# A fused attention and two-MLP kernel: the second four units of the first group take their decays from stored sums of log a

## The chip, the cores and the metric

The kernel runs on one core of one Trainium2 chip. The metric is the device time of a run in microseconds (us). Three runs of the kernel before were timed; the median counts. A profiled execution, with a time of its own, gives the trace.

## The reference, cut to what matters

The input goes through attention with a decay, then through two MLPs.

```python
# x: (4, 8, 768, 32)   a: (4, 8, 768)   B, C: (4, 8, 768, 16)
log_a = np.log(np.clip(a, 1e-06, 1.0))
for c in range(nc):                                # chunks of 32
    cum = np.cumsum(la, axis=-1)
    L = np.exp(cum[:, :, :, None] - cum[:, :, None, :]) * causal
    M = einsum('bhin,bhjn->bhij', Cc, Bc) * L
    y[:, :, sl] = M @ xc + einsum('bhin,bhnd->bhid', Cc, state) * exp(cum)
    state = exp(sum(la)) * state + sum_j Bx        # Bx decayed from j to the chunk's end
x = y.transpose(0, 2, 1, 3).reshape(3072, 256)
h = np.maximum(np.maximum(x @ w1, x @ w2), x @ w3)  # 256 -> 768
x = h @ w_out                                       # 768 -> 256
h = x @ w_in                                        # 256 -> 2048, then P(h)/Q(h)
out = g @ w_out                                     # 2048 -> 256
```

The kernel works in chunks of 128 (`CH`), which gives the same values.

## The kernel before, in words

The sequence of 768 is cut into six groups of 128 (`NG`). A group holds eight units (`NU`): a unit u is one batch and one half of the heads, that is four heads with a 128 x 128 block each, laid side by side as 128 x 512. For each unit TensorE makes the decay exponents d (`d_mm`), ScalarE takes their exponential e, TensorE makes the products s of C and B for a pair of units (`s_mm`), VectorE multiplies s and e to m (`m_op`), and TensorE multiplies m by x into y (`y_intra`). After the third y of a group the state is made (`state`), and from the second group on the old state is added (`y_inter`), behind a product p of the stored sums (`prep`).

The exponents come in two ways. In the first group (units 0 to 7) VectorE multiplies a triangle by log a into a tile `tl` of float32, and TensorE multiplies another triangle by it: a float32 product of 128 x 512. In all later groups the sums of log a up to each place, which ScalarE and VectorE made once as three bfloat16 parts (`cs`), are stored in DRAM (`cum_d`) and loaded back by `load_cum` into one of two tiles `lr`: its fixed part `lrc` (192 KB of ones, minus ones and zeros) is loaded once for each tile, and four small loads bring a group's sums, one of 24 KB for `rd` and three of 16 KB for `ld`. Then one bfloat16 product of 128 x 512 gives the exponents. Three more small loads fill `re` for p. Both ways begin with a bfloat16 product of the mask `trib`.

Beside the attention, 20 pieces of weights of 512 KB each are loaded into three buffers `wraw` and turned from float64 words to a high and a low float32r part: two instructions on ScalarE, three on VectorE, two half-sized on GpSimd, one copy on ScalarE, two half-sized on GpSimd. Eight further pieces (`wo2`) follow. The MLPs need these parts; their products are float32r triples (`mm3`).

A planner (`Plan`) sets the order on every engine: each operation is recorded with a cost, and the list is put out in an order that follows from these costs, from due times (`at`) and from rings of buffers. So each engine runs one fixed list in order. `FIRST` names loads whose due time is set ahead of all others, in its own order. All loads and stores go through SyncE's queue (SPq), in one order, and take eight completion semaphores in turn: an entry of the queue is issued only when the eighth entry ahead of it has landed. A weight piece is also held until its buffer is free, which the third VectorE instruction of the piece three earlier ends. When the attention's last operation has been put out (`second`), its buffers are given to the MLPs, and they begin (L650 to L652).

In the timeline, d is at L488 (mask) and L490 (sums), tl at L494, e at L504, s at L477, m at L509, y at L520, the state at L555 and L566, p at L455, the weights' instructions at L246 to L262, the loads at L283 and L241.

Of the kernel before, what the change touches and what calls it, by code (L numbers as in the profile page):

```python
# [9 lines left out]
F32 = mybir.dt.float32  # L10
# [18 lines left out]

OL = 6
LEAD = 3
HV, HL = "HAHP", "HHKK"
WARM = 9
PIECE = 2.6
FIRST = ["a", "t", "b0", "z0", "n0", "x0", "w1"]
KD = DM // 128
NU = 2 * NB
F1 = DF1 // 128  # L40
# [10 lines left out]
class Plan:  # L51
# [16 lines left out]
    def op(self, engine, cost, fn, reads=(), writes=(), at=None, behind=()):  # L68
        i = len(self.ops)
        deps, after = set(), {w for t in behind for w in t.writers}  # L70
        for t in reads:
            assert (t.writers or t.given) and not t.closed
            deps.update(t.writers)
            t.readers.append(i)
        for t in writes:
            assert not t.closed
            if t.first is None:
                t.first = i
                if t.before and not t.before.given:
                    after.add(t.before.first)  # L80
                if t.prev:
                    t.prev.closed = True
                    deps.update(t.prev.writers + t.prev.readers)
            deps.update(t.writers + t.readers)
            t.writers.append(i)
        deps.discard(i)
        after.discard(i)
        self.ops.append((engine, cost, fn, [t for t in writes if t.first == i], deps, after, at,
                         self.phase))
# [67 lines left out]
def decay_attention_max_moe_rational_moe(  # L157
# [113 lines left out]
    op = plan.op  # L271
# [144 lines left out]
    op("act", 0.21, lambda: act.activation(out=wrev, in_=pw.t[:, 0:192], func=AF.Exp), [pw], [wrev_t])  # L416
    load(lambda: cum_d.rearrange("p q r i -> r (p q) i"), cs.rearrange("r p q i -> r (p q) i"), [cum_t], [cs_t], kb=295)

    for i in (1, 0):
        op("dve", 0.5, lambda i=i: dve.memset(lr[i][64:128].bitcast(F32), 0.0), [], [lr_t[i]])  # L420
        load(lambda i=i: lr[i][0:64], lrc, [lr_t[i]], kb=197, nm=f"l{i}")
    load(lambda: co_raw, coef, [co_t, own_t], kb=68)

    def load_cum(g):
        q, i, j = g // 3, g % 2, g % 3
        load(lambda: rd[i][0:24], cum_d[:, q].rearrange("p (g u f) i -> p g u (f i)", u=NU, g=3)[:, j],
             [rd_t[i]], [cum_t, lr_t[i]], kb=25)
        for p in range(3):
            load(lambda p=p: ld[i][24 + 4 * p:28 + 4 * p],
                 cum_d[p, q].rearrange("(g u f) j -> g f u j", u=NU, g=3)[j], [ld_t[i][p]], [cum_t, lr_t[i]], kb=16)  # L430
        for p in range(3):
            load(lambda p=p: re[i][8 * p:8 * p + 8].rearrange("h (b i) -> h b i", b=NB),
                 cum_d[p, q].rearrange("(g b h) i -> g h b i", b=NB, g=3)[j], [re_t[i][p]], [cum_t], kb=16)

# [16 lines left out]
    def prep(g):  # L451
        if g:
            p0 = new("pd", "d", 2)
            book(("p0", g), 0.22)
            op("pe", 0.22, lambda: pe.matmul(p0.t, sel, re[g % 2], start=True, stop=True),  # L455
               [sel_t, *re_t[g % 2]], [p0], when["p0", g])
            e0[g] = new("s2", "e0", 2)
            op("act", 0.59, lambda: act.activation(out=e0[g].t, in_=p0.t, func=AF.Exp), [p0], [e0[g]])
            op("pool", 1.4, lambda: pool.tensor_tensor(out=ctg[g].t, in0=ctg[g].t, in1=e0[g].t, op=ALU.mult),
               [e0[g]], [ctg[g]])  # L460
        if g < NG - 1:
            op("dve", 0.8, lambda: dve.tensor_tensor(
                out=bg[g].t, in0=bg[g].t,
                in1=wrev[:, 32 * g:32 * g + 32].rearrange("j (u f) -> j u f", f=4)[:, :, None, :].to_broadcast(
                    [128, NU, NS, 4]), op=ALU.mult),
               [wrev_t], [bg[g]])
# [15 lines left out]
    def d_mm(u):  # L482
        g, k = divmod(u, NU)
        t = new("pd", "d", 2)

        def mm(w, x):

            pe.matmul(t.t.rearrange("j (f i) -> j f i", f=4), trib[:, 0],  # L488
                      trib[:, 1:2].to_broadcast([128, 4, CH]), start=True, stop=False)
            pe.matmul(t.t, w(), x(), start=False, stop=True)  # L490
        if g == 0:

            tl = new("s2", "tl", 2)
            op("dve", 0.78, lambda: dve.tensor_tensor(  # L494
                out=tl.t.rearrange("t (f i) -> t f i", f=4), in0=tri_s[:, 0:1, :].to_broadcast([128, 4, CH]),
                in1=la[:, 4 * u:4 * u + 4, None].to_broadcast([128, 4, CH]), op=ALU.mult), [tri_t, la_t], [tl])
            book(("d", u), 1.08)
            op("pe", 1.08, lambda: mm(lambda: tri_s[:, 1, :], lambda: tl.t), [tri_t, trib_t, tl], [t], when["d", u])
        else:
            book(("d", u), 0.46)  # L500
            op("pe", 0.46, lambda: mm(lambda: ld[g % 2][:, k], lambda: rd[g % 2]),
               [trib_t, lr_t[g % 2], rd_t[g % 2], *ld_t[g % 2]], [t], when["d", u])
        e_t[u] = e = new("s4", "e", 4)
        op("act", 0.59, lambda: act.activation(out=e.t, in_=t.t, func=AF.Exp), [t], [e])  # L504
# [88 lines left out]
    for g in range(2):  # L593
        load_s(g)
        load_v(g)
    prep(0)
    load_cum(1)
    for s in range(NS_ALL + LEAD + 3):
        if s < NS_ALL:
# [368 lines left out]
```

## Time and profile before

| | |
|---|---|
| median of 3 runs | 578.93 us (577.61 to 580.32) |
| profiled execution: its time | 579.21 us |
| profiled execution: span from first to last instruction | 577.3 us |
| TensorE (PE) busy | 556.8 us, 96% |
| VectorE (DVE) busy | 511.9 us, 89% |
| GpSimd (POOL) busy | 440.6 us, 76% |
| ScalarE (ACT) busy | 435.3 us, 75% |
| attention (until the first MLP product) | 0 to 100.4 us |

The profiled execution's own time lies 1.9 us above its span and 0.3 us above the median of the runs. PE is TensorE's matmuls, PEld its weight loads, SPq the queue of SyncE. Matmuls overlap: a matmul of 128 x 512 shows 0.38 to 0.39 us of busy time, but the next one starts sooner than that, so the time that one takes is read from start to start.

### The profile page before, as it was taken

Reading aid. Unit: us, or ns where it says so; the run is one execution under the profiler, and the core shown is the slowest. Engines: PE = TensorE matmul, PEld = TensorE weight load, DVE = VectorE, ACT = ScalarE, POOL = GpSimd, SP = SyncE. Lnnn points to the kernel's source line nnn. Section 1 sums busy time; section 2 is a strip of 40 time slices with the busy share of each in tenths; the row PEclk is TensorE's granted clock in tenths of the full one; section 3 lists DMA queues with packets and bytes.
Section 4 is the critical chain, followed back from the end, with each engine's and each line's share of the span. In section 5 each row is a group of like instructions: output and inputs, shape, how many; then the busy total and the mean of one; then the engine's idle time right before and its main releaser. Section 6 shows DMA issues by size and latency. Waiting matters only on the chain.

```text
span 577.3 us, 8164 instructions
## 1 busy us (share of the span) xinstructions
PE 556.8 (96%) x2747; PEld 411.2 (71%) x2758; DVE 511.9 (89%) x777; ACT 435.3 (75%) x756; POOL 440.6 (76%) x410
## 2 busy tenths in 40 slices
PE   8989989989999999999999999999999999999997
PEld 3333433768787788888888888888888888886563
DVE  7888979777999999998889988898898889988996
ACT  4677768556888878878788787778777877778883
POOL 1756767887989967778677877687777997869883
PEclk9999999999999999999999999999999999999999
DMA  6877864533000000101000010000000010000000
GB/s 216 243 270 238 237 233 148 182 110 109 1 1 2 18 20 0 37 1 38 0 1 37 1 33 6 0 20 18 1 1 1 0 37 0 1 1 36 2 0 36
DMA packets 19047, 33.71 MB, mean 58 GB/s; under 512 B 3526, under 2 KB 4030, under 8 KB 19006
## 3 DMA queue, kind: packets, MB, share of 16 engines
q1 hardware_dynamic: 19003, 33.20, 17.9%
q8 instruction: 21, 0.34, 0.2%
q14 instruction: 23, 0.16, 0.1%
HBM read 27.27 MB, written 5.91 MB: 57 GB/s over the span
## 4 chain that ended last, share of the span: by engine, by line
PE 53%; DVE 17%; POOL 17%; issue 4%; ACT 4%; DMA 3%; SPq 2%; POOLq 0%; ACTq 0%; DVEq 0%
PE pg L650 7%; PE pg L652 7%; PE pg L651 6%; PE ph L650 5%; PE ph L652 5%; PE ph L651 5%; PE po L652 4%; PE po L650 4%; PE po L651 4%; POOL glo L853 2%; PE s L477 2%; DMA wraw<-in_w_dram 2%; POOL v L819 2%; POOL hlo L295 2%; DVE pr L845 2%
## 5 line engine op out<-in xcount | busy, mean ns | idle before, releaser
L853 POOL TENSOR_TENSOR glo<-w,ghi 128x512 fp32r<-128x512 f32 x80 | 105.5, 1319 | 16.2 <-ACT ghi L196 16.1
L650 PE MATMUL pg<-xhi,w_hi 128*128 128x512 f32 x202 | 79.1, 392 | 2.8 <-DVE xa L732 2.2
L652 PE MATMUL pg<-xhi,w_lo 128*128 128x512 f32 x202 | 78.8, 390 | 0.0
L651 PE MATMUL pg<-xlo,w_hi 128*128 128x512 f32 x202 | 78.7, 390 | 0.0
L840 ACT ACTIVATE pr<-v,qc 128x512 f32<-128x512 f32 x83 | 57.4, 693 | 22.2 <-DVE v L826 11.3
L295 POOL TENSOR_TENSOR hlo<-xa,hhi 128x512 fp32r<-128x512 f32 x36 | 49.5, 1376 | 26.0 <-ACT hhi L196 25.9
L258 POOL TENSOR_TENSOR wa<-wa,we 128x256 uint32<-128x256 uint32 x56 | 44.2, 800 | 32.9 <-DVE wa L253 32.9
L196 ACT ACTIVATE ghi<-w 128x512 fp32r<-128x512 f32 x80 | 50.4, 630 | 23.9 <-PE po L652 14.2
L650 PE MATMUL ph<-yhi,win_hi 128*128 128x512 f32 x160 | 62.7, 392 | 1.7 <-DVE w L838 1.5
L651 PE MATMUL po<-glo,wo_hi 128*128 128x512 f32 x160 | 62.4, 390 | 0.4 <-POOL glo L853 0.4
L652 PE MATMUL ph<-yhi,win_lo 128*128 128x512 f32 x160 | 62.3, 390 | 0.0
L650 PE MATMUL po<-ghi,wo_hi 128*128 128x512 f32 x160 | 62.3, 390 | 0.0
L652 PE MATMUL po<-ghi,wo_lo 128*128 128x512 f32 x160 | 62.3, 390 | 0.0
L651 PE MATMUL ph<-ylo,win_hi 128*128 128x512 f32 x160 | 62.3, 389 | 0.0
L845 DVE SCALAR_TENSOR_TENSOR pr<-w,co,pr 128x512 f32<-128x512 f32 x83 | 61.9, 746 | 0.0
L819 POOL TENSOR_TENSOR v<-t,v 128x512 f32<-128x512 f32 x44 | 58.1, 1320 | 2.8
L842 DVE SCALAR_TENSOR_TENSOR v<-v,pr 128x512 f32<-128x512 f32 x83 | 56.2, 677 | 2.2 <-ACT pr L841 2.2
L847 DVE SCALAR_TENSOR_TENSOR w<-v,pr 128x512 f32<-128x512 f32 x83 | 56.3, 678 | 0.4
L841 ACT ACTIVATE pr<-pr 128x512 f32<-128x512 f32 x86 | 50.5, 587 | 0.9
L732 DVE TENSOR_TENSOR xa<-xa,pg 128x512 f32<-128x512 f32 x67 | 45.5, 679 | 2.3 <-PE pg L652 2.1
L650 PEld LDWEIGHTS pg<-xhi,w_hi 128*128 128x128 f32 x202 | 37.9, 188 | 12.1 <-DVE xa L732 3.1
L837 POOL TENSOR_TENSOR w<-w,t 128x512 f32<-128x512 f32 x20 | 25.9, 1293 | 24.0 <-DVE v L826 22.1
(167 smaller groups left out, 1485.1 us busy)
## 6 DMA issues: line engine op xcount, KB each, us to landing
wraw<-in_wo_dram SPq DMA_DIRECT2D x11, 512.0 KB
wraw<-in_w_dram SPq DMA_DIRECT2D x9, 512.0 KB
wraw<-in_win_dram SPq DMA_DIRECT2D x8, 512.0 KB
xn<-in_xn_dram SPq DMA_DIRECT2D x6, 512.0 KB
out_dram<-ob SPq DMA_DIRECT2D x12, 256.0 KB
xt_d<-xo SPq DMA_DIRECT2D x10, 256.0 KB
xst<-xt_d SPq DMA_DIRECT2D x10, 256.0 KB
bt<-in_bz_dram SPq DMA_DIRECT2D x6, 256.0 KB
```

Source lines behind the costliest of these rows:

```text
L196: act.activation(out=o, in_=i, func=AF.Copy)
L295: lambda: e.tensor_tensor(out=lo.t, in0=src(), in1=hi.t.bitcast(F32), op=ALU.subtract),
L650: pe.matmul(dst, wh, hi, start=first, stop=False)
L651: pe.matmul(dst, wh, lo, start=False, stop=False)
L652: pe.matmul(dst, wl, hi, start=False, stop=last)
L819: pop(1.23, lambda: pool.tensor_tensor(out=f(v), in0=f(t1), in1=f(v), op=ALU.mult), [t1], [v])
L840: aop(0.62, lambda: act.activation(out=f(r), in_=f(v), func=AF.Ln, bias=qc), [v], [r])
L841: aop(0.48, lambda: act.activation(out=f(r), in_=f(r), func=AF.Exp, scale=-1.0), [], [r])
L842: dop(0.61, lambda: dve.scalar_tensor_tensor(out=f(v), in0=f(v), scalar=QC, in1=f(r), op0=ALU.add, op1=ALU.mult), [r], [v])
L845: dop(0.61, lambda: dve.scalar_tensor_tensor(out=f(r), in0=f(w), scalar=c(0), in1=f(r), op0=ALU.add, op1=ALU.mult), [w], [r])
L847: dop(0.61, lambda: dve.scalar_tensor_tensor(out=f(w), in0=f(v), scalar=2.0, in1=f(r), op0=ALU.subtract, op1=ALU.mult), [v, r], [w])
L853: pop(1.23, lambda: pool.tensor_tensor(out=f(lo), in0=f(w), in1=f(hi).bitcast(F32), op=ALU.subtract), [w, hi], [lo])
```

## The change

Units 0 to 3 keep the triangle's product. Units 4 to 7 of the first group take the stored sums, as all later groups do: `load_cum(0)` is called, with due times ahead of others ("r0" in `FIRST`), and without the `re` loads, which the first group has no use for. The fixed part for the first group's tile, "l0", is put ahead of the first group's bn. The two memsets of `lr` move from VectorE to GpSimd, and the order of the two tiles is turned.

```diff
+ND = 4
-FIRST = ["a", "t", "b0", "z0", "n0", "x0", "w1"]
+FIRST = ["a", "t", "b0", "z0", "l0", "n0", "x0", "w1", "r0"]
...
-    for i in (1, 0):
-        op("dve", 0.5, lambda i=i: dve.memset(lr[i][64:128].bitcast(F32), 0.0), [], [lr_t[i]])
+    for i in (0, 1):
+        op("pool", 0.9, lambda i=i: pool.memset(lr[i][64:128].bitcast(F32), 0.0), [], [lr_t[i]])
         load(lambda i=i: lr[i][0:64], lrc, [lr_t[i]], kb=197, nm=f"l{i}")
...
     def load_cum(g):
         load(lambda: rd[i][0:24], cum_d[:, q].rearrange("p (g u f) i -> p g u (f i)", u=NU, g=3)[:, j],
-             [rd_t[i]], [cum_t, lr_t[i]], kb=25)
+             [rd_t[i]], [cum_t, lr_t[i]], kb=25, nm=f"r{g}" if not g else None)
         for p in range(3):
             load(lambda p=p: ld[i][24 + 4 * p:28 + 4 * p],
-                 cum_d[p, q].rearrange("(g u f) j -> g f u j", u=NU, g=3)[j], [ld_t[i][p]], [cum_t, lr_t[i]], kb=16)
-        for p in range(3):
+                 cum_d[p, q].rearrange("(g u f) j -> g f u j", u=NU, g=3)[j], [ld_t[i][p]], [cum_t, lr_t[i]], kb=16,
+                 nm=f"r{g}" if not g else None)
+        for p in range(3 if g else 0):
...
-        if g == 0:
+        if u < ND:
             tl = new("s2", "tl", 2)
...
     prep(0)
+    load_cum(0)
     load_cum(1)
```

Because a planner sets the order, the change moves instructions on all engines. First SyncE's queue, from the load of the second group's bt on; `lr_125` is the first group's tile in the change, `lr_126` and `cz_135` are the second group's. Before:

```order
L283 DMA bt<-in_bz_dram 128x512
L283 DMA cz_135<-in_ct_dram 32x512
L283 DMA re_128<-cum_d 8x4x128 x3
L241 DMA wraw<-in_w_dram 128x2x512
L283 DMA cz_135<-in_ct_dram 32x512 x3
L283 DMA xn<-in_xn_dram 128x1024
L283 DMA lr_126<-cum_d 24x1x512
L283 DMA lr_126<-cum_d 4x8x128 x3
L283 DMA bn<-in_bn_dram 128x512
L283 DMA ct<-in_ct_dram 128x512
L241 DMA wraw<-in_w_dram 128x2x512
```

With the change:

```order
L285 DMA bt<-in_bz_dram 128x512
L285 DMA cz_135<-in_ct_dram 32x512
L285 DMA lr_125<-cum_d 24x1x512
L285 DMA lr_125<-cum_d 4x8x128 x3
L243 DMA wraw<-in_w_dram 128x2x512
L285 DMA re_128<-cum_d 8x4x128 x3
L285 DMA lr_126<-cum_d 24x1x512
L285 DMA lr_126<-cum_d 4x8x128 x2
L243 DMA wraw<-in_w_dram 128x2x512
L285 DMA lr_126<-cum_d 4x8x128
L285 DMA cz_135<-in_ct_dram 32x512 x3
L285 DMA xn<-in_xn_dram 128x1024
```

Four new loads stand ahead of the fourth weight piece. The fifth piece now stands ahead of the last three loads of `cz_135`, of xn, bn and ct; before it stood behind them all.

On TensorE, the middle of the first group, before: products of tl for units 3 to 5 between s and y.

```order
L477 MATMUL s<-cz_134,bt 128x512 x2
L488 LDWEIGHTS trib
L488 MATMUL d<-trib 128x512
L490 MATMUL d<-tl,tri_s 128x512
L488 LDWEIGHTS trib
L488 MATMUL d<-trib 128x512
L490 MATMUL d<-tl,tri_s 128x512
L520 MATMUL y<-m,xn 32x128 x8
L488 LDWEIGHTS trib
L488 MATMUL d<-trib 128x512
L490 MATMUL d<-tl,tri_s 128x512
L477 MATMUL s<-cz_134,bt 128x512 x2
```

With the change, from unit 3's product on:

```order
L493 MATMUL d<-tl,tri_s 128x512
L523 MATMUL y<-m,xn 32x128 x4
L480 MATMUL s<-cz_134,bt 128x512 x2
L523 MATMUL y<-m,xn 32x128 x4
L480 MATMUL s<-cz_134,bt 128x512 x2
L523 MATMUL y<-m,xn 32x128 x8
L480 MATMUL s<-cz_134,bt 128x512 x2
L491 LDWEIGHTS trib
L491 MATMUL d<-trib 128x512
L493 LDWEIGHTS lr_125
L493 MATMUL d<-lr_125 128x512
```

All of the first group's s and y of units 0 to 3 now come ahead of unit 4's d.

Last, TensorE where the second group's first s (it reads `cz_135`) is reached. Before, three d of the second group and y of units 4 to 6 stood ahead of it:

```order
L490 MATMUL d<-lr_126 128x512
L520 MATMUL y<-m,xn 32x128 x4
L488 LDWEIGHTS trib
L488 MATMUL d<-trib 128x512
L490 LDWEIGHTS lr_126
L490 MATMUL d<-lr_126 128x512
L520 MATMUL y<-m,xn 32x128 x4
L488 LDWEIGHTS trib
L488 MATMUL d<-trib 128x512
L490 LDWEIGHTS lr_126
L490 MATMUL d<-lr_126 128x512
L520 MATMUL y<-m,xn 32x128 x4
```

With the change it follows the first group's last d (unit 7), ahead of p and of every d of the second group:

```order
L523 MATMUL y<-m,xn 32x128 x4
L491 LDWEIGHTS trib
L491 MATMUL d<-trib 128x512
L493 LDWEIGHTS lr_125
L493 MATMUL d<-lr_125 128x512
L480 MATMUL s<-cz_135,bt 128x512 x2
L458 LDWEIGHTS sel
L458 MATMUL d<-re_128,sel 128x512
L523 MATMUL y<-m,xn 32x128 x4
```

## Rows read from the trace of the kernel before

**Rows 1.** Stretches: length, busy PE, PEld, DVE, ACT, POOL, clock, DMA share, GB/s
```profile
0.00:100.00 100.00, 88.65 (x745) 37.26 (x756) 86.57 (x151) 70.61 (x127) 61.96 (x78) 1.00 0.73 228
100.00:160.00 60.00, 55.83 (x240) 44.58 (x241) 47.28 (x64) 39.83 (x71) 51.58 (x57) 0.97 0.29 98
160.00:540.00 380.00, 379.07 (x1657) 310.35 (x1656) 346.44 (x511) 299.97 (x514) 301.68 (x251) 1.00 0.04 12
```

**Rows 2.** Timeline of TensorE: a float32 unit and the instruction behind it, then a bfloat16 unit
```profile
10.95 0.39 PE L488 MATMUL d<-trib 128*128 128x512 bf16 x1
11.18 1.02 PE L490 MATMUL d<-tl,tri_s 128*128 128x512 f32 x2
12.13 1.13 PE L477 MATMUL s<-cz,bt 64*128 64x512 f32 x4
...
24.78 0.39 PE L488 MATMUL d<-trib 128*128 128x512 bf16 x1
...
25.32 0.43 PE L520 MATMUL y<-m,xn 128*32 128x128 f32 x8
```

**Rows 3.** Timeline of VectorE: tl of units 4 to 7, and one memset of lr
```profile
4.78 0.70 DVE L420 MEMSET lr<- 64x768 f32 x1 [0.21 <-issue]
...
13.03 0.68 DVE L494 TENSOR_TENSOR tl<-tri_s,la 128x512 f32<-128x512 f32 x1
...
14.84 2.06 DVE L494 TENSOR_TENSOR tl<-tri_s,la 128x512 f32<-128x512 f32 x2
...
18.09 1.22 DVE L494 TENSOR_TENSOR tl<-tri_s,la 128x512 f32<-128x512 f32 x1
```

**Rows 4.** Timeline of TensorE at the start: the warming products ahead of the first real ones
```profile
2.29 4.02 PE L376 MATMUL y<-zero 128*128 128x512 bf16 x9 [2.29 <-DVE zero L372]
...
6.11 1.06 PE L399 MATMUL s<-tri_s,la 128*96 128x128 f32 x4
```

**Rows 5.** Timeline of SyncE's queue: start and time of issue (landing comes later)
```profile
10.23 1.04 SPq L241 DMA_DIRECT2D wraw<-in_w_dram  x2
...
14.81 0.40 SPq L241 DMA_DIRECT2D wraw<-in_w_dram  x1
16.89 2.12 SPq L283 DMA_DIRECT2D cz<-in_ct_dram  x3
...
22.69 0.38 SPq L241 DMA_DIRECT2D wraw<-in_w_dram  x1
...
69.25 0.35 SPq L283 DMA_DIRECT2D lr<-cum_d  x1
```

**Rows 6.** Waits of SyncE's queue: in total, times, longest
```profile
SPq L283 <- DMA wraw<-in_w_dram: 4.7, 4, 2.5
```

**Rows 7.** Timeline of PEld: p of the fifth group, after the load at 69.25
```profile
70.46 0.09 PEld L455 LDWEIGHTS <-sel 24*128 24x128 bf16 x1 [0.76 <-DMA lr<-cum_d]
```

**Rows 8.** Timeline: the second group's first s, and the standstill behind it
```profile
26.57 1.13 PE L477 MATMUL s<-cz,bt 64*128 64x512 f32 x4
...
28.98 0.66 ACT L249 ACTIVATE we<-wraw 128x512 uint32<-128x512 uint32 x1 [2.71 <-DMA wraw<-in_w_dram]
...
30.18 0.38 PE L488 MATMUL d<-trib 128*128 128x512 bf16 x1 [1.07 <-ACT e L504]
```

**Rows 9.** Two stretches with that standstill, columns as in rows 1
```profile
25.00:30.00 5.00, 3.97 (x35) 1.28 (x35) 2.38 (x3) 2.29 (x5) 3.65 (x4) 1.00 0.94 225
30.00:35.00 5.00, 3.64 (x27) 1.31 (x26) 4.29 (x9) 4.08 (x9) 1.59 (x2) 1.00 0.57 199
```

**Rows 10.** Timeline of TensorE: its longest wait in the first MLP
```profile
125.80 0.50 PE L650 MATMUL pg<-xhi,w_hi 128*128 128x512 f32 x1 [1.94 <-DVE xa L732]
```

**Rows 11.** The three stretches behind that wait, columns as in rows 1
```profile
126.00:128.00 2.00, 2.00 (x8) 1.58 (x8) 0.64 (x2) 1.45 (x3) 1.58 (x2) 0.79 0.21 71
128.00:130.00 2.00, 2.00 (x7) 1.52 (x6) 1.56 (x3) 0.63 (x1) 1.31 (x2) 0.50 0.50 192
130.00:132.00 2.00, 2.00 (x9) 1.64 (x8) 1.81 (x4) 1.81 (x4) 0.38 (x1) 0.86 0.00 0
```

## The prediction

> **What bounds the kernel now.** I read first the stretches of the span. After 160 us TensorE is busy for 379.07 of 380 us, and the change touches nothing there: what it is worth is decided earlier. The attention (0 to 100 us) has 88.65 us of PE, 86.57 of DVE, and a DMA share of 0.73; the stretch behind it, where the first MLP runs while weights are still being converted, has 55.83 of 60 us at a mean clock of 0.97 [rows 1]. So in both stretches TensorE is nearly full, and what shortens its work or its waits there shortens the kernel, if no other wait takes the place. The timeline then gives the cost of a unit on PE, and the waits and the DMA queue show what is late.
>
> **The float32 products.** A float32 unit takes PE from 10.95 to 12.13, start to start: 1.18 us. A bfloat16 unit takes it from 24.78 to 25.32: 0.54 us [rows 2]. Four units change from the one to the other: 4 x (1.18 - 0.54) = 2.6 us of PE are taken away. Since PE is the engine that is nearly full, I count them whole: **-2.6**.
>
> **The tl of units 4 to 7 on VectorE.** They take 0.68 + 2.06 + 1.22 = 3.96 us between 13.03 and 19.31 [rows 3]. That time goes to m and to the weights, which share VectorE; I count nothing for it beside the term above, because both engines work side by side and PE keeps the longer list. Its use shows below, in the weights.
>
> **The memsets.** Two of 0.70 us leave VectorE [rows 3]. They are hidden both before and after: PE runs its warming products from 2.29 to 6.31, and its first real product starts at 6.11 [rows 4]. On GpSimd they stand ahead of the first weight piece, whose data cannot have come. Nothing; if PE had no warming to do, VectorE's 1.4 us would be the most that it gains.
>
> **The loads.** Four new loads go into SyncE's queue, and what matters is whom they push. Before, the fourth weight piece was issued at 14.81 [rows 5]. With the change it stands eight entries behind the third piece, so it is issued when that one has landed. The issue of cz at 16.89 shows when: it stood in that place before, and the queue's waits for a weight piece are 4.7 us in 4 times [rows 5, 6]. So the fourth piece goes from 14.81 to about 16.9. On ScalarE the e of unit 6 stands behind it; what PE loses by that it does not lose at cz, below. The 192 KB of l0, moved ahead of bn, delay the transfers behind it by up to 192 KB / 228 GB/s = 0.8 us [rows 1]; I count nothing, because the same bytes leave the fullest stretch, 25 to 30 us with a DMA share of 0.94 [rows 9].
>
> From 16.9 on: 0.4 for that issue, six entries at about 0.5 (between the 0.35 of the lr load and 2.12 / 3 = 0.71 of a cz load), and the fifth piece is issued at about 20.3, where it was 22.69 [rows 5]. Behind it an lr load and the three cz: the last cz starts to issue at 20.3 + 0.4 + 0.5 + 2 x 0.71 = 22.6. Before, these three began at 16.89.
>
> **The new wait.** TensorE's first s of the second group needs all of cz. It stood at 26.57 [rows 8]. In the new order three d (0.54 each), p and one y (at most 0.43 each, by the y [rows 2]) come behind it instead of ahead, 2.5 us in all; with the 2.6 saved, PE could be there at 26.57 - 2.6 - 2.5 = 21.5. Behind this s in PE's list stand p, unit 6's y and all d of the second group, so a wait here stops everything. From issue to landing: the shortest that a row shows is 69.25 to 70.46, 1.2 us, for a load of 16 KB in a quieter stretch [rows 5, 7]; the longest is the fifth piece, 22.69 to 28.97 (28.98 is when ScalarE went on), 6.3 us for 512 KB in the fullest stretch [rows 5, 8]. I take 1.5, near the short end, because cz is 64 KB and its flight starts in a thinner queue. It lands at 24.1 and PE waits 2.6 us: **+2.6** (bounds: 0, if VectorE or ScalarE keep PE from arriving before 24.1; 22.6 + 6.3 - 21.5 = 7.4). The new loads for unit 4 come before this point: the fourth of them waits for the second piece, issued at 10.23 + 0.5, and each microsecond that PE loses on them is one that it does not lose at cz; so they cost nothing of their own.
>
> **The standstill that goes.** Before, PE lost 10 - 3.97 - 3.64 = 2.39 us between 25 and 35 us [rows 9]. ScalarE waited 2.71 us for the fifth piece, the e behind it came late, and PE waited for e [rows 8]. Issued 2.4 us earlier, with the same flight, the piece costs ScalarE 0.3 instead of 2.71: **-2.0** of these 2.39 (bounds: 0, -2.4).
>
> **The pieces left for the first MLP.** By the instruction lists, one more piece has been through VectorE when the first MLP begins (20, where it was 19, of 28). Between 100 and 160 us PE loses 60 - 55.83 = 4.17 us while nine pieces are converted [rows 1], about 0.46 each: **-0.5** (bounds: 0, and the whole 4.17 with its clock loss, below).
>
> **Sum:** -2.6 + 2.6 - 2.0 - 0.5 = -2.5 against the profiled execution's 579.21, which is 576.7; that execution lies 0.3 above the median of 578.93, so the runs should have their median at **576.4**.
>
> **The rivals.**
>
> *B: the long wait in the first MLP goes too.* PE waits 1.94 us at 125.80 for VectorE [rows 10], and then the granted clock is 0.79, 0.50 and 0.86 for two microseconds each [rows 11]: the lower of the two levels, 1.2 GHz, for about 3.4 of 6 us, a loss of 0.42 + 1.0 + 0.28 = 1.7. Where the wait falls depends on which weight instructions stand ahead of one max on VectorE, and that list is shuffled. For it: one piece less is left. Against: nothing in the rows says that the shuffle helps. Without wait and clock loss: 576.4 - 3.6 + 0.5 = 573.3 (the 0.5 is then counted already).
>
> *C: the gain is handed back.* PE reaches the first MLP 2 us earlier, but the weights' low and high parts are made by VectorE, ScalarE and GpSimd, and if these set the pace between 100 and 160 us (GpSimd is busy 51.58 of 60 us [rows 1]), PE waits there for what it won. For it: the waits of that stretch are waits for VectorE, not for attention. Against: VectorE has 3.96 us less to do. Time: 578.9.
>
> *D: the loads come too late, and the kernel is slower.* The three cz now stand behind the fifth weight piece, 512 KB, instead of ahead of it. If they land only when that piece's flight allows, after 6.3 us like it, PE waits 7.4 instead of 2.6: +4.8. Such a wait is longer than the 1.94 after which the clock fell [rows 10, 11]; a fall like that one adds 1.7. Together 576.4 + 6.5 = 582.9. It decides, that is the kernel gets slower than before, from a wait of 2.6 + 2.5 = 5.1 us on, with cz landing at 26.6. For it: the DMA share of 0.94 in 25 to 30 us. Against: waits of about 1.1 us in the standstill (1.07 at 30.18 [rows 8]) leave the clock at 1.00 [rows 9], and the piece is then alone with small loads.
>
> The Trainium skill's page "TensorE: Matmul & The Clock Gate", section "HAM oscillation — how this bites in real kernels", says that waits for DMA between bursts of matmuls send the array back to its slow clock, burst after burst. By that rule D's clock loss follows from the wait itself, and the sum with D's wait alone would be 581.2, with it 582.9. The trace agrees in one place, behind the 1.94 us [rows 10], and shows no fall behind the shorter waits [rows 8].
>
> **How the numbers follow.** Chances: the forecast 0.45, B 0.18, C 0.20, D 0.17. Around the forecast the terms on cz and on the standstill move by 1 to 2 us, so its own range is 574.5 to 578.5. About 0.5%, 2.9 us, is what a measurement of this kernel can tell from no change. Faster than 576.0: B, and somewhat over half of the forecast's case (0.24 of 0.45), 0.42. Slower than 581.8: D, and a trace of C, 0.18. Between: 0.40. The range of 571.5 to 582.0 leaves out the best of B and the worse half of D.
>
> **What would show it.** In the profile after: four float32 units instead of eight, a fifth piece issued at about 20 us, the last cz at about 22.6, PE waiting at the second group's first s for a load for 2 to 3 us, no wait of ScalarE of 2.7 us for the fifth piece, the first MLP product at about 98.4 instead of 100.4, and 3.7 us or less of PE idle between its start and 60 us later. I am wrong if PE waits at unit 4's d for the new loads by more than 1 us, if the wait at cz is above 5 us, or if a new wait above 1.9 us stands in the first MLP with a low clock behind it.

## The result, and the profile after

The changed kernel takes **585.58 us** (median of 6 runs, 583.56 to 586.47) against 578.76 us of the kernel before (6 runs): a ratio of 1.0102, 95% interval 1.008 to 1.0124, so it is about 5.9 us slower. (The ratio compares all runs; the two medians alone differ by 6.8 us.) The forecast was 576.4 us; the range ended at 582.0. The profiled execution took 583.56 us, with a span of 581.8: it is the fastest of the six, so its trace shows less than the whole of the loss.

First the stretches after; columns as in [rows 1], which they answer to.

```profile
0.00:100.00 100.00, 84.11 (x688) 33.23 (x688) 79.41 (x139) 67.64 (x123) 62.53 (x80) 0.98 0.71 227
100.00:160.00 60.00, 56.09 (x286) 42.83 (x282) 47.25 (x65) 39.43 (x68) 50.67 (x56) 0.97 0.30 100
160.00:540.00 380.00, 379.17 (x1663) 311.72 (x1664) 345.19 (x511) 300.45 (x511) 298.67 (x249) 1.00 0.03 12
...
105.99:165.99 60.00, 56.75 (x240) 44.99 (x237) 47.44 (x65) 39.94 (x70) 52.70 (x58) 0.97 0.29 97
```

Behind 160 us nothing has changed, as expected. The last row is the 60 us from the first product of the first MLP on. Ahead of 100 us PE is busy 4.5 us less than in [rows 1]. The shorter products are one part of that; the other is work of the attention that now falls behind 100 us, for the first product of the first MLP starts at 105.99 us, where it was 100.36. PE has less to do and idles more. The timeline of TensorE after shows the two waits that the prediction spoke of:

```profile
20.21 0.38 PE L493 MATMUL d<-lr 128*128 128x512 bf16 x1 [2.31 <-DMA lr<-cum_d]
...
27.34 1.13 PE L480 MATMUL s<-cz,bt 64*128 64x512 f32 x4 [2.82 <-DMA cz<-in_ct_dram]
28.40 0.38 PE L458 MATMUL d<-re,sel 24*128 24x512 bf16 x1
...
46.42 0.58 PE L491 MATMUL d<-trib 128*128 128x512 bf16 x1 [1.27 <-DVE st L576]
...
68.22 0.43 PE L523 MATMUL y<-m,xn 128*32 128x128 f32 x8 [1.87 <-DVE m L512]
...
105.99 0.50 PE L654 MATMUL pg<-xhi,w_hi 128*128 128x512 f32 x1
...
130.55 0.50 PE L654 MATMUL pg<-xhi,w_hi 128*128 128x512 f32 x1 [1.92 <-DVE xa L736]
```

The first is unit 4's d, which waits 2.31 us for the new loads; the second is the second group's first s, which answers to [rows 8] and waits 2.82 us for cz. Two more stand far behind them, at 46 and 68 us, and are waits for VectorE; the last row answers to [rows 10]. The queue of SyncE after answers to [rows 5]:

```profile
18.24 0.40 SPq L243 DMA_DIRECT2D wraw<-in_w_dram  x1
...
21.89 0.40 SPq L243 DMA_DIRECT2D wraw<-in_w_dram  x1
22.33 0.35 SPq L285 DMA_DIRECT2D lr<-cum_d  x1
22.73 2.59 SPq L285 DMA_DIRECT2D cz<-in_ct_dram  x3
...
52.35 4.52 SPq L285 DMA_DIRECT2D xt_d<-xo  x2
...
63.27 0.37 SPq L285 DMA_DIRECT2D bn<-in_bn_dram  x1
```

The fourth piece of weights is issued at 18.24 (forecast 16.9) and the fifth at 21.89 (forecast 20.3), so the last cz lands 3.2 us later than forecast, and PE is 3 us late to want it. The last two rows are the stores of the second group's output, at which the queue stood, and the load of the fifth group's bn far behind them; in the kernel before that load was issued at 50.31. And VectorE's products bn of the second and third group, then its rows from 64 to 68 us:

```profile
29.61 0.69 DVE L465 TENSOR_TENSOR bn<-bn,wrev 128x512 f32<-128x512 f32 x1 [1.55 <-DMA bn<-in_bn_dram]
...
40.32 0.70 DVE L465 TENSOR_TENSOR bn<-bn,wrev 128x512 f32<-128x512 f32 x1 [1.52 <-DMA bn<-in_bn_dram]
...
64.64 1.10 DVE L255 SCALAR_TENSOR_TENSOR wa<-wraw,wa 128x512 uint32<-128x512 uint32 x1
66.62 0.94 DVE L465 TENSOR_TENSOR bn<-bn,wrev 128x512 f32<-128x512 f32 x1 [0.88 <-DMA bn<-in_bn_dram]
67.48 0.68 DVE L512 TENSOR_TENSOR m<-s,e 128x512 f32<-128x512 f32 x1
```

VectorE stands 0.88 us at the fifth group's bn, whose load was issued at 63.27, then works on it, and the m that PE waits for comes after both. At the third group's bn it stands 1.52 us; at the fourth's, at 53.52, it does not stand at all. In the whole stretch from 5 to 110 us VectorE's and SyncE's waits (total, times, longest) hold

```profile
DVE bn L465 <- DMA bn<-in_bn_dram: 4.0, 3, 1.6
```

```profile
SPq L285 <- ACT xo L198: 17.2, 6, 7.7
```

Of the 17.2 us, 3.7 lie ahead of the load at 63.27. Before, VectorE waited once for a bn, the third group's, for 3.3 us up to 30.70, and the queue's waits for xo were 6.8 us, the longest 3.0. The clock, in 5-us stretches, falls once in the attention:

```profile
25.00:30.00 5.00, 2.67 (x17) 0.88 (x17) 3.29 (x6) 2.11 (x5) 1.11 (x2) 1.00 0.76 262
30.00:35.00 5.00, 4.19 (x31) 1.48 (x31) 3.54 (x5) 4.67 (x9) 4.99 (x6) 1.00 0.67 208
...
45.00:50.00 5.00, 3.54 (x15) 0.91 (x14) 5.00 (x10) 2.94 (x5) 3.87 (x5) 0.66 0.52 166
65.00:70.00 5.00, 3.13 (x20) 1.16 (x20) 4.12 (x7) 3.60 (x8) 4.56 (x5) 1.00 0.96 294
```

The first two answer to [rows 9]: PE idles 10 - 2.67 - 4.19 = 3.14 us there, where it was 2.39. At 45 to 50 us it runs much of the time at the lower level, 1.2 GHz. The kernel before has no such stretch ahead of 100 us.

### The profile page after: what moved, and what is told of

Read it like the earlier page. It is cut to its first block, busy times and chain, and to the rows that moved or that the text cites. A ratio compares the mean times of both kernels' runs of the same rounds, so it can differ in the third digit from the quotient of the medians.

```text
span 581.8 us, 8159 instructions
## 1 busy us (share of the span) xinstructions
PE 557.2 (96%) x2754; PEld 409.6 (70%) x2754; DVE 507.5 (87%) x771; ACT 437.0 (75%) x756; POOL 441.6 (76%) x412
## 4 chain that ended last, share of the span: by engine, by line
PE 52%; POOL 18%; DVE 16%; DMA 5%; issue 4%; ACT 4%; SPq 1%; POOLq 0%; DVEq 0%; ACTq 0%
PE pg L654 7%; PE pg L656 7%; PE pg L655 7%; PE ph L654 5%; PE ph L656 5%; PE ph L655 5%; PE po L654 4%; PE po L656 4%; PE po L655 4%; POOL glo L857 3%; POOL hlo L297 2%; POOL v L823 2%; POOL wa L260 1%; DVE pr L849 1%; DVE v L846 1%
```

## The experiments

All ratios are to runs of the kernel before on the same chip (13 to 26 of them in each group, medians 578.78 to 579.76 us); "forecast" means what stood on record before the run.

### First theory: the two waits on late loads

The theory took the prediction's own two places for the cause. In `cz_ahead` three loads go ahead of the fourth weight piece on SyncE's queue, with every compute engine's list as in the changed kernel; in `r0_early` the first group's sums are replaced by zeros from `lrc`, loaded ahead of the store of `cum_d`; `both_early` has both. (The loads got names for this, and a list of moves, what ahead of what, is applied to the order that the planner has made; `both_early` is shown, the other two have one half each.)

```diff
+    plan.moves = [("r0", "cum"), ("z1", "w4")]
     plan.emit(second)
...
-             cum_d[:, q].rearrange("p (g u f) i -> p g u (f i)", u=NU, g=3)[:, j],
+             cum_d[:, q].rearrange("p (g u f) i -> p g u (f i)", u=NU, g=3)[:, j] if g else
+             lrc[0:24, 1024:1536],
```

Expected of `cz_ahead`:

> The changed kernel with the lists of PE, VectorE, ScalarE and GpSimd kept as they are; only the three cz_135 loads move in SyncE's queue, from behind the fifth weight piece to ahead of the fourth. Theory 1 (late loads cost the time: 2.31 us of PE at unit 4's d, 2.82 at the second group's first s, and what follows): the 2.82 goes, the first MLP product comes at about 103.2 instead of 105.99, the time is about 582.8 (585.6 before this move). Theory 2 (the new lists on the engines cost the time, and the waits for loads only show where it is lost): another wait takes its place, first MLP product at 105 or later, 585.

Of `r0_early`:

> The changed kernel with the lists of the four compute engines kept; the four small loads of the first group's sums read a block of zeros of the fixed input instead of the stored sums, so that they need not wait for the store, and stand ahead of the store in SyncE's queue. It leaves out the round trip of the first group's sums. Theory 1: no wait at unit 4's d, the fourth and fifth weight piece and cz come up to 2.3 us sooner, so the wait at the second group's first s shrinks too; first MLP product 101.5 to 103.7, time 581 to 583.3. Theory 2: 105 or later, 585.

Of `both_early`:

> Both moves together: the first group's sums replaced by zeros that are loaded early (the round trip is left out), and the three cz loads ahead of the fourth weight piece; lists of the compute engines as in the changed kernel. Theory 1: both waits gone, first MLP product at 101 or earlier, time 580.5 or less; if the prediction's terms held otherwise (2.6 us of PE saved) even 576. Theory 2: the lists cost it, first MLP product at 104 or later, time 584.

Measured: 585.22 us, ratio 1.0105 (1.0079 to 1.013); 583.9 us, 1.0078 (1.0049 to 1.0108); 583.56 us, 1.0076 (1.0061 to 1.0091). With both waits gone, 5.1 us of waiting in the trace, the kernel gains only about 1.5 us by the ratios, whose intervals overlap, and its profiled run reaches the first MLP no earlier (107.32 us; that run took 583.88 us, about as long as the changed kernel's profiled run). The waits of TensorE from 5 to 110 us in `both_early` have no load of lr or cz any more, and their largest group is

```profile
PE y L533 <- DVE m L522: 7.1, 9, 3.1
```

where the changed kernel has 4.7 us in 9 times, the longest 1.9. Part of what PE wins early it waits for later, at m. As the main cause the theory falls: these waits are real, but something behind them sets most of the time. The kernel before has, in the same stretch,

```profile
PE y L520 <- DVE m L509: 1.6, 3, 0.8
```

`memset_only` is the kernel before with the two memsets on GpSimd:

```diff
-        op("dve", 0.5, lambda i=i: dve.memset(lr[i][64:128].bitcast(F32), 0.0), [], [lr_t[i]])
+        op("pool", 0.9, lambda i=i: pool.memset(lr[i][64:128].bitcast(F32), 0.0), [], [lr_t[i]])
```

> The kernel before with the two lr memsets on GpSimd instead of VectorE and nothing else changed (all other rows of all lists are the same). In the changed kernel the first d started at 6.57 instead of 7.60. If the memsets did that: first d at about 6.6, first MLP product up to 1 us earlier, 577.8 to 578.8. If it came from elsewhere: first d at 7.6 and 578.8.

Measured: 579.16 us, 1.0006 (0.9986 to 1.0026). The memsets are worth nothing that can be measured.

### The order apart from the work

Two runs cross the two. `old_order` keeps the lists of all compute engines of the kernel before, row by row; only units 4 to 7 read `lr`, tl is not made for them, and SyncE gets the first group's loads. `old_work` keeps all lists of the changed kernel, makes tl and the float32 products for units 4 to 7, and leaves the four loads out.

```diff
-            op("pe", 1.08, lambda: mm(lambda: tri_s[:, 1, :], lambda: tl.t), [tri_t, trib_t, tl], [t], when["d", u])
+            op("pe", 1.08, lambda: mm(*((lambda: tri_s[:, 1, :], lambda: tl.t) if u < 4 else
+                                        (lambda: ld[0][:, k], lambda: rd[0]))), [tri_t, trib_t, tl], [t], when["d", u])
```

> All instructions of the four compute engines stand in the order of the kernel before; units 4 to 7 take the stored sums (float32 product and tl gone), and SyncE's queue gets the new loads where the changed kernel has them (early load of the first lr ahead of co_raw, four loads of sums ahead of the first re). Theory of the work (the added waits on loads cost the time): as slow as the changed kernel or near it, 583 to 586 us. Theory of the order (the planner's new order of weights, attention and loads costs the time): not slower than before, 575 to 580 us, first product of the first MLP before 100.5 us.

> All instructions stand in the order of the changed kernel, but units 4 to 7 make tl and the float32 product again and the four loads of the first group's sums are left out. Theory of the work: back to 577 to 580 us. Theory of the order: still slow, 583 to 588 us, first product of the first MLP later than 104 us.

Measured: `old_order` 581.31 us, 1.0038 (1.0022 to 1.0053); `old_work` **585.85 us**, 1.0105 (1.0085 to 1.0124). The order with the old work costs as much as the whole change, as the theory of the order had forecast. And the new work in the old order does not gain: it loses 0.4%, between the two forecasts for it. Its timeline of TensorE shows one long wait,

```profile
18.90 0.54 PE L502 MATMUL d<-lr 128*128 128x512 bf16 x1 [3.77 <-DMA lr<-cum_d]
```

with a granted clock of 0.90 and 0.76 in the stretches 15 to 20 and 20 to 25 us. The old order comes to unit 4's d sooner than the new one, so the loads are later for it.

### Is it the loads on SyncE's queue?

`old_nd6` is `old_order` with only units 6 and 7 on the stored sums (`u < 6`), so that TensorE wants the loads later.

> The compute engines' order of the kernel before; units 4 and 5 keep the triangle's product and only units 6 and 7 take the stored sums, so that their loads are in before TensorE wants them. No wait for lr over 0.5 us; two products of 0.54 instead of 1.18 us: 577.5 to 579.5 us if the 3.8 us wait at unit 4 with the low clock behind it was the whole loss of the run with the old order and four such units; 580 to 582 us if the new loads cost by their place on SyncE's queue.

Measured: 581.46 us, 1.0037 (1.0022 to 1.0051). The wait for the first group's loads is 0.21 us. First two rows of the kernel before, the second group's loads on SyncE's queue and its p on TensorE, then the same of this run:

```profile
19.70 2.00 SPq L283 DMA_DIRECT2D lr<-cum_d  x4
...
23.42 0.38 PE L455 MATMUL d<-re,sel 24*128 24x512 bf16 x1
```

```profile
22.16 1.96 SPq L286 DMA_DIRECT2D lr<-cum_d  x4
...
23.43 0.38 PE L467 MATMUL d<-re,sel 24*128 24x512 bf16 x1
...
26.41 0.38 PE L502 MATMUL d<-lr 128*128 128x512 bf16 x1 [1.78 <-DMA lr<-cum_d]
```

TensorE is at p as early as before, but the second group's loads start 2.5 us later, because four loads more stand ahead of them, and now PE waits for these. The clock is 0.75 in 25 to 30 us. So the loads cost by their place on the queue, also where TensorE hardly waits for these loads themselves.

`old_none` is `old_order` without the four loads; `lr` then holds the zeros of its first load, and the first group's sums are taken as zero. `old_pool` does the whole computation and issues the four loads from GpSimd, right behind the store of `cum_d`. `after_none` is the changed kernel, in its order, without them.

```diff
-        nc.sync.dma_start(out=rd[0][0:24], in_=cum_d[:, 0].rearrange("p (g u f) i -> p g u (f i)", u=NU, g=3)[:, 0])
+        nc.gpsimd.dma_start(out=rd[0][0:24], in_=cum_d[:, 0].rearrange("p (g u f) i -> p g u (f i)", u=NU, g=3)[:, 0])
         for p in range(3):
-            nc.sync.dma_start(out=ld[0][24 + 4 * p:28 + 4 * p],
+            nc.gpsimd.dma_start(out=ld[0][24 + 4 * p:28 + 4 * p],
```

> The compute engines' order of the kernel before, units 4 to 7 with products from lr, but the four loads of the first group's sums are left out (lr then holds the zeros of its first load, so that the first group's sums are taken as zero). Theory of the queue (four loads of 1.9 us on SyncE's queue hold what stands behind them): 575.5 to 577.5 us, no wait for lr over 0.5 us before 30 us. If the shorter products give nothing even without the loads: 578.5 us or more.

> The same with the four loads issued by GpSimd, right behind the store of cum_d and ahead of its first conversion, so that nothing on SyncE's queue stands behind them; the whole computation is done. Theory of the queue: 576 to 578.5 us, faster than before. If the loads cost by the engines' transfer time or by TensorE's wait for them: 580 us or more.

> The changed kernel and its order with the four loads left out (the first group's sums taken as zero). Theory that the planner's new order costs most by itself: 582 to 585 us. Theory of the queue alone: 576 to 579 us.

Measured: `old_none` **579.05 us**, 0.9989 (0.9968 to 1.001); `old_pool` 583.27 us, 1.0062 (1.0038 to 1.0085); `after_none` **584.21 us**, 1.0083 (1.0055 to 1.0111).

`old_none` falls short of the 575.5 to 577.5 us that the theory of the queue forecast: without any load in the way, four products of 0.54 instead of 1.18 us and four tl less give 0.6 us (by the interval, between 1.9 gained and 0.6 lost). ScalarE's first weight instruction shows one reason; the first row is of the kernel before, the others are of `old_none`.

```profile
11.06 0.67 ACT L246 ACTIVATE wa<-wraw 128x512 f32<-128x512 f32 x1 [1.24 <-DMA wraw<-in_w_dram]
```

```profile
12.08 0.66 ACT L249 ACTIVATE wa<-wraw 128x512 f32<-128x512 f32 x1 [2.99 <-DMA wraw<-in_w_dram]
...
13.84 0.38 PE L499 MATMUL d<-trib 128*128 128x512 bf16 x1 [1.48 <-ACT e L516]
...
19.14 0.38 PE L499 MATMUL d<-trib 128*128 128x512 bf16 x1 [1.11 <-ACT e L516]
...
20.78 1.99 SPq L286 DMA_DIRECT2D lr<-cum_d  x4
...
22.79 0.38 PE L466 MATMUL d<-re,sel 24*128 24x512 bf16 x1
```

The first lr's load of 192 KB, now early, goes ahead of the first weight piece's data; ScalarE stands at that piece, the e's behind it come late, and PE waits for them twice. Of the 2.6 us, 0.6 are left at p (22.79 against 23.42). PE then waits 2.02 us for loads of the second group, whose four lr loads start at 20.78 us (before: 19.70), although no load has been added. (The profiled run is the longest of its twelve, 576.0 to 581.4 us; what is read from it is confined to these rows.)

`old_pool` shows that another queue does not help:

```profile
13.47 0.75 POOL L433 DMA_DIRECT2D lr<-cum_d  x1 [10.88 <-DMA cum_d<-cs]
14.22 1.75 POOL L435 DMA_DIRECT2D lr<-cum_d  x3
...
20.70 0.59 PE L506 MATMUL d<-lr 128*128 128x512 bf16 x1 [5.86 <-DMA lr<-cum_d]
```

GpSimd waited until 13.47 for the store of `cum_d` and issued until 15.97; PE went on at 20.70, after 5.86 us, with a DMA share of 0.99 in 15 to 20 us. In the Trainium skill, "DMA: Bandwidth & Descriptors", section "Issuing engines are not separate DMA queues", says that transfers from all issuing engines share the same 16 engines, and that a second issuing engine saves issue time alone. This trace agrees: the loads were used at 20.70 us, no sooner than from SyncE's queue (18.90 in `old_order`).

### What in the order

Three runs tested the count of weight pieces that stand ahead of the attention's m on VectorE (7 ahead of the sixteenth m where it was 6). `w_back` puts loads and conversions of pieces 4 to 15 later in the changed kernel's order, `w_fwd` puts them earlier in the order before, and `l0_behind` names the first lr's load behind the first piece, so that the planner's own order has 6 again. The first part of the diff is `w_back` (`w_fwd` has -4.5), the second `l0_behind`.

```diff
+        for x, p in self.piece.items():
+            when[x] += 4.5 * (4 <= p < 16)
...
+        order.sort(key=lambda x: when[x])
...
-FIRST = ["a", "t", "b0", "z0", "l0", "n0", "x0", "w1", "r0"]
+FIRST = ["a", "t", "b0", "z0", "n0", "x0", "w1", "l0", "r0"]
```

> The changed kernel with its order kept, except that loads and conversions of weight pieces 4 to 15 stand 4.5 us (of the planner's time, about one piece) later among the attention's instructions, as far as their dependences allow. Theory of the weights (one or two pieces more ahead of m and e are the loss): 578 to 582 us, first product of the first MLP before 102.5 us. Theory of the attention's own order (s of later units ahead of earlier d's, loads in another order): 584 to 587 us.

> The kernel before with its order kept, except that loads and conversions of weight pieces 4 to 15 stand 4.5 us (about one piece) earlier, as far as dependences allow. Theory of the weights: 582 to 586 us, waits for VectorE's m or ScalarE's e of 3 us or more between 20 and 70 us. Theory of the attention's own order: 578 to 581 us.

> The changed kernel with one entry of the table moved: the first lr's load is named behind the first weight piece, not ahead of the first bn; the planner orders anew, and 6 weight pieces stand ahead of the sixteenth m instead of 7, as before. Theory of the weights: 578 to 582 us. If the loss is in TensorE's own order (s of units 4 to 7 ahead of the first product that waits for lr) it stays at 584 to 587 us.

Measured: 592.82 us, 1.0238 (1.0212 to 1.0264); 586.84 us, 1.0137 (1.0103 to 1.0171); 584.98 us, 1.0095 (1.0068 to 1.0122). Moving the pieces back makes the changed kernel worse, moving them ahead makes the kernel before worse, and six pieces instead of seven ahead of the sixteenth m change nothing that can be measured (ahead of the 24th, `l0_behind` still has nine, where it was eight before and is ten in the changed kernel). `w_back` and `l0_behind` speak against the theory of the count. `w_fwd` came out on its side, but a shift by one piece in either direction puts other loads late (2.4 us for cz in `w_back`, 3.06 us of one wait for cz in `w_fwd`), so that these two runs do not isolate the count.

`sp_fix` changed SyncE's queue alone: bn of two groups and ct of one earlier, two stores of the output later. `sp_fix_all` has `both_early` and a later first lr as well.

```diff
+    plan.moves = [("n3", "c3"), ("n4", "o1"), ("c4", "o1"), ("o1", "e5")]
     plan.emit(second)
```

> The changed kernel with the order of the compute engines kept; on SyncE's queue bn of the fourth and fifth group and ct of the fifth go ahead of loads that wait for buffers, and the two stores of the second group's output go behind the fifth group's loads. If the order costs through SyncE's queue (bn landed late at 66 to 67 us, the queue stood 17.2 us at stores that waited for ScalarE's xo): 578 to 582 us, the wait for m at 65 to 70 us gone. If it costs through the weight pieces ahead of m and e on VectorE and ScalarE: 583 to 586 us. Theory of the work: 585 us.

> As the run before, with the three cz loads ahead of the fourth weight piece, the early lr behind the first weight piece, and the first group's sums replaced by loaded zeros (no round trip through DRAM). No load should hold TensorE, at the start or later. If late loads are all of the loss: 576 to 579 us. If weight pieces ahead of m and e cost by themselves: 582 to 585 us.

Measured: 589.95 us, 1.0179 (1.0159 to 1.0198), and 593.39 us, 1.0235 (1.0212 to 1.0257), slower than every forecast. These two edits made waits of their own and say little of the order. In `sp_fix`:

```profile
SPq L293 <- PE d L566: 11.4, 2, 7.5
```

```profile
70.14 0.60 ACT L204 ACTIVATE xo<-y 128x512 f32<-128x512 f32 x1 [7.75 <-DMA xt_d<-xo]
```

An earlier bn makes the whole queue stand until TensorE has done with the buffer's old content, and a later store holds the two `xo` buffers, at which ScalarE then stood for 7.75 us with all e's behind it.

`cost_only` is the kernel before with one number of the planner changed, the cost of four products, so that it writes another order for the same work.

```diff
-            op("pe", 1.08, lambda: mm(
+            op("pe", 1.08 if u < 4 else 0.46, lambda: mm(
```

> The kernel before with all its work; only the planner's cost of the first group's last four products is 0.46 instead of 1.08, so that it writes another order (one weight piece more ahead of the attention from the 24th m on). No load is added and no product shortened. If the loss of the changed kernel lies in having been ordered anew: 581 to 586 us. If it lies in the first lr's early load and what follows from it: 578 to 580 us.

Measured: 582.03 us, 1.0034 (1.001 to 1.0058): a new order alone costs some 2 us (by the interval 0.6 to 3.4), without a new load or a shorter product. It is not the changed kernel's order.

The last two runs move three instructions of VectorE, the bn products of the third to fifth group, behind two to five of the m's that they stood ahead of. In VectorE's list the three stand behind 13, 19 and 24 m's in the changed kernel and behind 15, 22 and 29 in these two runs; in the kernel before they stood behind 8, 25 and 27, so that the new order had moved the third group's back and the other two forward. Nothing else moves on any engine. `bn_late` is the changed kernel, `bn_late_none` is `after_none`.

```diff
+        for x in self.bn:
+            when[x] += 6
...
+            if g > 1:
+                plan.bn.append(len(plan.ops))
             op("dve", 0.8, lambda: dve.tensor_tensor(
                 out=bg[g].t, in0=bg[g].t,
```

> The changed kernel; only on VectorE three instructions stand elsewhere, the products bn of groups 2 to 4, each behind two to four of the m's that it stood ahead of. If VectorE standing at a bn that has not landed (4.0 us in three waits in the changed kernel, 1.5 of it at 65 to 67 us) and TensorE behind it is a main piece of the loss: 580 to 582.5 us, no wait of TensorE for m over 1.5 us at 64 to 70 us. If the time is given back elsewhere: 584.5 to 586.5 us.

> The same move in the changed kernel without the four loads of the first group's sums (taken as zero). If the bn's place is the main piece of what the new order costs: 577.5 to 580.5 us, against 584.2 without the move. If not: 583 us or more.

Measured: **581.81 us**, 1.005 (1.0034 to 1.0066), and **580.63 us**, 1.0021 (1.0005 to 1.0037). The first is in its forecast; the second misses its own by 0.1 us, but is far from "not". TensorE's timeline and two stretches in `after_none`:

```profile
67.23 0.42 PE L523 MATMUL y<-m,xn 128*32 128x128 f32 x8 [3.08 <-DVE m L512]
...
106.39 0.50 PE L654 MATMUL pg<-xhi,w_hi 128*128 128x512 f32 x1
```

```profile
65.00:70.00 5.00, 2.77 (x16) 0.79 (x16) 4.99 (x8) 3.05 (x7) 2.73 (x3) 0.88 0.85 283
70.00:75.00 5.00, 5.00 (x58) 2.81 (x58) 1.99 (x4) 2.98 (x6) 2.49 (x5) 0.78 0.39 108
```

and in `bn_late_none`:

```profile
64.90 0.42 PE L535 MATMUL y<-m,xn 128*32 128x128 f32 x8 [0.55 <-DVE m L524]
...
102.81 0.50 PE L666 MATMUL pg<-xhi,w_hi 128*128 128x512 f32 x1
```

```profile
65.00:70.00 5.00, 4.87 (x50) 1.82 (x52) 4.44 (x8) 3.65 (x7) 4.26 (x6) 1.00 0.94 281
70.00:75.00 5.00, 5.00 (x55) 2.48 (x55) 4.88 (x11) 4.12 (x7) 2.78 (x4) 1.00 0.77 266
```

The same y waits 0.55 instead of 3.08 us, and the clock behind it stays at its upper level. The first MLP starts at 102.81 instead of 106.39 us, 3.6 us sooner, which is what the medians show. What the move takes from in front of the m's is both the standing at loads (1.37 and 1.47 us at the third and fifth group's bn in `after_none`, none at the fourth's) and the products' own time; the two were not separated. The same move was not made in the kernel before. That the whole gain belongs to the new order is therefore argued: there PE waits only 1.6 us in all for m, where the changed kernel waits 4.7 and `after_none` 6.5.

The clock takes part in these differences. Each run has a mean granted clock on record: in the median 0.991 in the changed kernel, `after_none`, `old_nd6` and `old_pool`, 0.993 in `bn_late`, 0.994 in `old_none`, 0.995 in `bn_late_none`, and 0.996 to 0.997 in the kernel before. As an estimate, 0.005 to 0.006 of 580 us is 2.9 to 3.5 us: so much of the changed kernel's 5.9 us can be time at the lower level, 1.2 GHz, if TensorE had work throughout it, and up to 0.004 of 580, 2.3 us, of the 3.6 us that moving the bn's gives back without the loads. In the traces the lower level follows waits of PE (0.88 and 0.78 behind the 3.08 us above), so this is a part of what the waits cost and not a cause beside them; which wait brings a fall was not tested.

No version that was run is faster than the kernel before by more than its interval.

## Why the prediction was wrong

From the ratios, in us of 579. The products and tl, with the first lr's load early, in the old order: -0.6 (`old_none`). The new order beside that: 584.21 against 579.05 us, ratios 1.0083 and 0.9989, +5.4. The four loads in the new order: 1.0102 against 1.0083, +1.1, with intervals that overlap; in the old order 1.0038 against 0.9989, +2.8, with intervals apart. The sum, -0.6 + 5.4 + 1.1, is the measured +5.9, as it must be, since each step starts where the one before it ends.

- **The step that failed is the sum's end at 35 us.** The prediction followed the new order at two places, up to the standstill at 25 to 35 us, and took the attention behind it as unchanged. The order alone costs 5.4 us. Moving three bn products on VectorE gives 3.6 of them back (1.0083 against 1.0021; 3.0 with the loads in). They stand ahead of m's that TensorE needs, and the third and the fifth group's data land late: SyncE's queue, in order, issues them behind stores and loads that wait. That the queue is why they land late is read from the traces and was not shown by a run, since an earlier bn made the queue stand (`sp_fix`). The other 1.8 us of the order stay open: which of its rows they hang on was not found, and the intervals of `bn_late_none` and `old_none` just touch.
- **-2.6 for the products, "counted whole".** Measured with no new load of sums in the way: 0.6, together with the early lr's load. PE was the fullest engine of the attention on average, but at 13 to 23 us ScalarE's e's, behind weight data, set its pace in the profiled run. The two terms together came out 2 us short (the interval leaves 0.7 to 3.2), and how much of that is the products and how much the early load stays open.
- **The new loads, "nothing of their own".** Measured +1.1 to +2.8. The reason given, that a microsecond lost on them is not lost at cz, held for the one wait (PE came to cz 3 us later), but four loads more move all that follows on SyncE's queue, as `old_nd6` showed with a wait of only 0.21 us for the loads themselves. Unit 4's d waited 2.31 us, over the 1 us that the prediction named as the sign that it is wrong.
- **The first lr's 192 KB, "I count nothing".** They put the first weight piece about 1 us later, and PE waits at two e's (`old_none`); their price apart from the products was not measured.
- **+2.6 at cz.** The wait is there with 2.82 us. But taking it away gained nothing by itself (`cz_ahead`): its size was right, and it did not decide.
- **-2.0 for the standstill, -0.5 for the pieces.** In 25 to 35 us PE idles 3.14 us instead of 2.39. Of that, 27.34 - 25 = 2.34 is the wait at cz, so 0.8 is left beside it; and ScalarE waits for no weight piece from 19 to 36 us. The standstill is mostly gone, as forecast, and another wait took its place. In the first 60 us from the first MLP's start PE idles 60 - 56.75 = 3.25 us, where it was 4.17: -0.9, more than forecast, and under the 3.7 us that the prediction named as a sign.
- **The memsets**, counted at nothing: nothing (`memset_only`).
- **The rivals.** D ended on the right side, 582.9 us, but not by its mechanism: the wait at cz was under its 5.1 us and no low clock followed it. C said that the gain is handed back, and in the old order it was, in the attention and not in the first MLP. B did not happen: a wait of 1.92 us for VectorE stands at 130.55, with a granted clock of 0.50 in 132 to 134 us.

## What to carry to other kernels

Where a planner writes the order, a change of the work is two changes: build the old order with the new work and the new order with the old work, and time both before crediting or blaming either. Forecast an order by walking each in-order list to the stage's end, and at every instruction that reads a load ask when that load is issued on its own queue, because here three products ahead of the critical instructions, two of which stood at their data, cost more than the four shortened ones gave. A busy share of 0.89 over 100 us, the highest of all engines, does not say that shortening that engine's work at one place is worth its length: ask what the next instruction of it waited for just there.

## What the runs showed of the hardware that had not been expected

The length of a wait does not tell by itself whether TensorE's clock falls. In the changed kernel the wait of 2.82 us at 27.34 (PE is busy for 1.19 of the 4 us from 24 to 28) is followed by a granted clock of 1.00 in 25 to 30 and in 30 to 35 us; the wait of 1.27 us at 46.42 (PE is busy for 2.59 of the 4 us from 42 to 46) is followed by

```profile
46.00:48.00 2.00, 1.39 (x10) 0.31 (x9) 2.00 (x6) 1.63 (x3) 0.95 (x2) 0.61 0.22 70
48.00:50.00 2.00, 2.00 (x12) 0.51 (x4) 2.00 (x3) 1.26 (x3) 2.00 (x2) 0.54 0.56 146
```

the lower level, 1.2 GHz, most of the time. The page of the Trainium skill that the prediction cited, "TensorE: Matmul & The Clock Gate", section "HAM oscillation — how this bites in real kernels", describes a fall behind waits for loads that are longer than both of these. So the 2.82 us without a fall do not speak against it, and the fall behind 1.27 us is not a case that it describes. Nor is the one behind the 1.94 us of [rows 10], where the prediction saw the trace agree: both were waits for VectorE. And small loads took long in a full stretch: the four of 16 to 24 KB that GpSimd issued by 15.97 let PE go on 4.7 us later, at a DMA share of 0.99, where [rows 7] show 1.2 us for one of 16 KB in a quieter stretch.
